# Attention into a token-mixing MLP: how p and the small weights are loaded, the form of the scores in batch 2, and the order of the work

## The chip, the cores and the metric

The kernel runs on one core of a Trainium2 chip. The metric is the device time of one execution in microseconds, as the median of several runs; a profiled execution gives the trace beside it. Engines are called PE (matrix products), DVE (vector), ACT (activation), POOL (GpSimd) and SP (which only issues transfers here). Transfers are issued by SP, ACT and POOL and run on 16 DMA engines that all of them share.

## The reference, cut to what matters

```python
def attn(qq, kk, vv):                      # scale = 1 / sqrt(64)
    s = scale * qq @ kk.T
    a = exp(s - max(s)); a = a / sum(a)
    return a @ vv

p_packed = attn(p, k, v)                   # p: 8 x 8 x 32 x 64, q, k, v: 8 x 8 x 576 x 64
x = heads_side_by_side(attn(q, p_packed, p_packed))      # 8 x 576 x 512
wq, wk = x @ w_q, x @ w_k                  # 512 x 64 each
mixed = (wq @ wk.T / sqrt(64)) @ x         # per batch, 576 x 576 mixing of tokens
out = maximum(mixed, 0) @ w_out            # 512 x 512, fp32
```

All inputs and the output are fp32. 32 learned vectors per head (p) attend to the keys and values, and the 576 queries then attend to the 32 results.

## The kernel before

All eight batches go through the same steps; nothing loops. The text `ORDER` is a list of steps, written out by hand or by a planner, and the program walks it once: `NAME.batch.piece@engine=banks`. The engine is V (DVE), A (ACT) or P (POOL); what follows `=` are the PSUM banks. Each engine runs its own steps in the order of the text and waits only for what a step reads, or for a buffer or bank that is still in use; the order between engines in the text has no further meaning. There are four buffers each for the loads of q, k and v, three for most of the rest, two for the exponentials. POOL's queue also shows waits of an issue for the landing of the eighth issue before it.

The steps of one batch, with the lines of the profile:

- `LD.k`, `LD.q`, `LD.v` (L184, L191, L181): 576 KB each in bf16, cast from fp32 on the way by POOL's transfers; v goes in two halves. `LD.g0` and `LD.h0` are the halves of k in batch 0, `LD.q7` and `LD.r7` those of q in batch 7. `LD.O` is w_out, `LD.W0` and `LD.W1` are w_q and w_k, `LD.P0` to `LD.P3` the four quarters of p. `LD.P0`, `LD.P1` and both W are fp32 copies on SP's or ACT's queue.
- At the start `PC` casts the two fp32 quarters of p (L137), `PX` transposes p (L244), `PB` spreads it into a block form for batches 0 to 2 (`pblk`), `WC` casts the two weights into `wqk`, and `SET` fills constants: ones beside v (L215), zeros of `pblk` (L218), the mask (L220), an identity (`idf`, `aff`, `idb`), zeros of `aT` (L140) and of the tile `warm`. `WARM.n` is n matmuls on that tile (L616), fillers whose result nobody reads.
- `KT` transposes k on DVE (L244). `S1` gives the scores of p against k. For the batches in `DIAG` they come with the tokens on partitions (L281, 36 matmuls with `pblk`), and one `X1` (L299) takes the exponential; for the others they come with p on partitions (L291, 32 matmuls), `X1` is two instructions (L302), and `TE` transposes the result back in two instructions on DVE (L244).
- `PV` (L318) multiplies with v and sums; `RC` and `PP` (L323, L327) divide; `PT` transposes the result, `QV` transposes q in three pieces (0, 1: 512 columns each, 2: the rest). `QK` (L340) and `QKE` give w_k and w_q times the packed values, `QD` copies a part on POOL.
- `S2` (L379) gives the scores of the queries, `X2` (L384) their exponential, `RS` and `RR` (L400, L405) the sums and reciprocals, `AM` (L411) the product of both on DVE or POOL, `AT` and `AE` the transposed result. Pieces 0 and 1 are two groups of 128 tokens each, 2 is the last, 3 is the first four groups and 4 all five. Batches 0, 1 and 7 use 0, 1 and 2, the others 3 and 2 (4 for the sums).
- `WKQ`, `WE`, `GM`, `GE`, `Y`, `YE`, `MX`, `MR`, `RL`, `RLR`: the token mixing, folded into small products, and the relu. `OT` (L546) is the product with w_out, `OE` and `OEF` bring it out of PSUM, `ST` (L564, L566) and `STF`, `STH` store it from SP. Results wait in SBUF: the first store stands in the text near the end of batch 6.
- `HOLD.q7` is a transfer of a few bytes from the second half of batch 7's q into a tile that nobody reads (L576). It stands last.

The core of the walk, and the first waits of the two forms:

```python
for item in ORDER.split():
    name, _, bk = item.partition("=")
    name, _, eng = name.partition("@")
    f = name.split(".")
    if f[0] == "LD":
        load(f[1], eng)
    ...
    steps[f[0]](*[int(z) for z in f[1:]], eng, bk[0] if bk and len(bk) == 1 else bk)
```

Of the kernel before, what the change touches and what calls it, by code (L numbers as in the profile page):

```python
# [29 lines left out]
AM.2.3@V AM.2.2@V AT.2.3=7 AT.2.2=6 AE.2.3@V RL.1.1@A AE.2.2@V TE.3.1@V OE.0.1@A TE.3.0@V KT.4.2@V  # L30
MR.1=2,3 OT.0.1 WKQ.2.0=0,1 WKQ.2.2 RLR.1@A OE.0.0@A MX.1.0=2,3 WKQ.2.1 PV.3.0=6,7 PV.3.1 RC.3.1@V
RC.3.0@V PP.3.0@V PP.3.1@V WE.2.2@A RL.1.0@A PT.3@V OT.1.4=4 S1.4=0,1,6,7 OEF.1.4@A QK.3=2
OT.1.0=4,5 GM.2=3 X1.4.1@A QKE.3@A X1.4.0@A QV.3.1@V QV.3.0@V QV.3.2@V S2.3.2=6,7 GE.2@A X2.3.2@A
S2.3.3=0,1 Y.2=6,7 TE.4.1@V TE.4.0@V YE.2@V X2.3.3@A RS.3.4@V OT.1.1 MR.2=6,7 PV.4.0=2,3 OE.1.0@A
RLR.2@A PV.4.1 MX.2.0=0,1 MX.2.1=4,5 OT.1.2=6,7 RL.2.0@A RL.2.1@A RR.3.4@V RC.4.0@V RC.4.1@V OT.1.3
# [17 lines left out]
OT.5.4=6 S2.7.2=2,3 S2.7.1=0,1 S2.7.0=4,5 X2.7.2@A OEF.5.4@V RS.7.2@V GM.6=7 X2.7.1@A RR.7.2@V
RS.7.1@V GE.6@A X2.7.0@A RS.7.0@V RR.7.1@V RR.7.0@V AM.7.0@V AM.7.1@V OT.5.2=2,3 QK.7=7 Y.6=4,5
AM.7.2@P AT.7.2=0 OT.5.3 QKE.7@A AE.7.2@A YE.6@A QD.7@P OE.5.1@A MX.6.0=4,5 MX.6.1=0,1 OT.5.0=6,7
AT.7.0=2 AT.7.1=3 AE.7.0@A RL.6.1@V RL.6.0@V AE.7.1@A OT.5.1 WKQ.7.0=0,1 WKQ.7.2 WKQ.7.1 OT.6.0=2,3
WE.7.0@V WE.7.1@A OE.5.0@V GM.7=0 OT.6.1 GE.7@V OE.6.0@A Y.7=6,7 MR.6=0,1 YE.7@V RLR.6@V OT.6.2=4,5
MX.7.0=2,3 MR.7=0,1 MX.7.1=6,7 RLF.7.0.0@A RLF.7.1.1@A RLR.7@V OT.6.3 RLF.7.0.1@V RLF.7.1.0@V
# [590 lines left out]
```

## Time and profile before

| | us |
|---|---|
| median of 3 runs (109.5 to 110.06) | 109.88 |
| the profiled execution | 109.32 |
| its span, first to last instruction | 107.5 |
| first product of data (S1.0) starts | 11.18 |
| last load lands | 79.1 |
| first store issued | 78.44 |
| PE's last product of batch 7 ends, ACT's last copy starts | 102.9 |

The span is what the trace shows; the execution's own time has 1.8 us around it. Times inside the trace are counted from the span's start. A row of the trace's time line reads: start, length, engine, line, operation, what it writes and reads, shape and type, and in brackets how long the engine had been idle before it and who released it. Matmuls are pipelined: PE's rows overlap, and a row's length is longer than its share of PE's time (a matmul of 512 columns has rows of 380 ns and follows the one before by 216).

The inputs are loaded in 37 transfers by POOL and four by SP and ACT; 14 of the stores are 512 KB each. The loads of batches 0 to 2 are issued by 17.8 us, those of batch 7 between 63.2 and 66.3.

### The profile page before, as it was taken

What the parts mean: (1) busy time and instruction counts of PE and PEld (TensorE: products, weight loads), DVE (VectorE), ACT (ScalarE), POOL (GpSimd) and SP (SyncE); (2) the same over time, 40 slices, a digit from 0 to 9 for tenths busy, and PEclk for the clock granted to TensorE, in tenths of its full rate; (3) what the DMA queues carried; (4) which work ended last, traced back from release to release, by engine and by line L of the source; (5) the groups of instructions that cost most, each with busy time, mean ns of one, the idle gap of its engine ahead of it and who ended that gap; (6) DMA issues with size and microseconds to landing.
All of it is one profiled execution on the core that took longest, in us unless ns stands there. A gap on an engine that the chain in (4) does not pass through costs nothing.

```text
span 107.5 us, 3632 instructions
## 1 busy us (share of the span) xinstructions
PE 97.2 (90%) x1551; PEld 54.8 (51%) x1551; DVE 82.8 (77%) x177; ACT 68.9 (64%) x108; POOL 42.7 (40%) x65
## 2 busy tenths in 40 slices
...
GB/s 41 196 145 172 213 214 210 207 213 217 203 208 214 204 209 213 209 207 214 208 214 206 214 205 211 213 209 208 162 115 396 407 393 401 395 405 329 213 370 120
DMA packets 13376, 25.01 MB, mean 233 GB/s; under 512 B 1072, under 2 KB 6448, under 8 KB 13360
## 3 DMA queue, kind: packets, MB, share of 16 engines
...
q8 instruction: 12, 0.20, 0.7%
...
HBM read 30.15 MB, written 9.44 MB: 368 GB/s over the span
## 4 chain that ended last, share of the span: by engine, by line
PE 68%; DVE 18%; ACT 5%; issue 3%; POOL 1%; DVEq 0%; ACTq 0%; POOLq 0%
PE ps L546 23%; PE ps L616 16%; PE ps L379 5%; PE ps L318 5%; PE ps L281 3%; ACT e L299 3%; PE ps L498 3%; DVE rs L400 3%; PE ps L425 3%; DVE kT L244 2%; PE ps L473 2%; PE ps L452 2%; DVE qT L244 2%; PE ps L291 2%; DVE aT L137 2%
## 5 line engine op out<-in xcount | busy, mean ns | idle before, releaser
L546 PE MATMUL ps<-wout,relu 128*128 128x512 bf16 x124 | 31.0, 380 | 0.6 <-DVE pp L327 0.6
L616 PE MATMUL ps<-o 128*128 128x512 bf16 x79 | 20.7, 410 | 3.6 <-DVE o L140 2.4
L411 POOL TENSOR_TENSOR a<-e,rr 128x256 bf16<-128x256 f32 (+2 forms) x11 | 13.1, 1196 | 23.4 <-DVE rr L405 23.4
L133 ACT ACTIVATE o<-ps 128x1024 f32<-128x1024 f32 (+2 forms) x18 | 15.7, 880 | 4.3 <-PE ps L546 3.9
L546 PEld LDWEIGHTS <-relu 128*128 128x128 bf16 x124 | 10.6, 98 | 11.9 <-issue 2.6
L384 ACT ACTIVATE e<-ps 128x256 f32<-128x256 f32 (+2 forms) x19 | 11.1, 620 | 7.7 <-PE ps L379 7.3
L509 ACT ACTIVATE relu<-ps 128x1024 bf16<-128x1024 f32 (+1 forms) x12 | 14.1, 1219 | 2.5 <-PE ps L498 2.1
L616 PEld LDWEIGHTS <-o 128*128 128x128 bf16 x79 | 7.6, 104 | 12.9 <-issue 3.9
L181 POOL DMA_DIRECT2D v_sb<-in_v_dram x16 | 10.1, 642 | 6.4 <-DMA q_sb<-in_q_dram 2.2
L244 DVE STREAM_TRANSPOSE qT<-q_sb 128x512 uint32<-128x512 uint32 (+1 forms) x24 | 12.4, 544 | 0.2 <-DMA q_sb<-in_q_dram 0.2
L244 DVE STREAM_TRANSPOSE kT<-k_sb 128x1152 uint32<-128x1152 uint32 (+1 forms) x9 | 11.0, 1224 | 1.3 <-DMA k_sb<-in_k_dram 1.2
L400 DVE TENSOR_REDUCE rs<-e 128x16 f32<-128x512 f32 (+2 forms) x13 | 10.8, 846 | 0.7 <-ACT e L384 0.6
L133 ACT ACTIVATE wkq<-ps 128x896 bf16<-128x896 f32 (+1 forms) x8 | 6.2, 776 | 3.7 <-PE ps L447 2.1
L318 PE MATMUL ps<-v_sb,e 64*64 64x192 bf16 x288 | 8.0, 245 | 0.1
L302 ACT ACTIVATE e1T<-ps 128x576 bf16<-128x576 f32 x10 | 6.4, 653 | 1.8 <-PE ps L291 1.8
L323 DVE RECIPROCAL rec<-ps 64x2 f32<-64x2 f32 x16 | 2.6, 164 | 6.2 <-PE ps L318 5.9
L244 DVE STREAM_TRANSPOSE e<-e1T 128x576 bf16<-128x576 bf16 x10 | 7.1, 744 | 0.0
L318 PEld LDWEIGHTS <-e 64*64 64x64 bf16 x288 | 6.0, 106 | 1.8 <-issue 1.0
L452 PE MATMUL ps<-aT,pqk 128*128 128x256 bf16 (+1 forms) x48 | 6.9, 246 | 0.0
L379 PE MATMUL ps<-ppT,qT 64*128 64x64 bf16 x320 | 6.4, 190 | 0.1
L379 PEld LDWEIGHTS <-qT 64*128 64x128 bf16 x320 | 5.4, 94 | 2.1 <-issue 1.1
L447 PE MATMUL ps<-pqk,aT 128*128 128x64 bf16 x80 | 6.1, 193 | 0.4 <-DVE aT L137 0.2
...
## 6 DMA issues: line engine op xcount, KB each, us to landing
...
v_sb<-in_v_dram POOLq DMA_DIRECT2D x16, 288.0 KB, 12.9
q_sb<-in_q_dram POOLq DMA_DIRECT2D x7, 576.0 KB, 13.4
k_sb<-in_k_dram POOLq DMA_DIRECT2D x7, 576.0 KB, 13.8
...
k_sb<-in_k_dram POOLq DMA_DIRECT2D x2, 288.0 KB, 6.9
q_sb<-in_q_dram POOLq DMA_DIRECT2D x2, 288.0 KB, 12.2
```

The lines of the kernel that those rows point to most:

```text
L133: nc.scalar.activation(o, i, COPY)
L181: nc.gpsimd.dma_start(v_bufs[b % NL][halves(i), 1:5], src)
L244: nc.vector.transpose(o, i)
L318: nc.tensor.matmul(T["pv", b][halves(cc), i, cc * Dh:(cc + 3) * Dh], lhsT, rhs, start=n == 0, stop=n == R - 1, skip_group_check=True)
L379: nc.tensor.matmul(ps[:, y, t - t0, i], lhsT, rhs, start=e == 0, stop=e == 1)
L384: nc.scalar.activation(e2[:, t0:t1].rearrange("a t (i y n) -> a y (t i) n", i=2, y=2), T["s2", b, c].rearrange("a y t i n -> a y (t i) n") ...
L400: nc.vector.tensor_reduce(rs[:, t0 * H:t1 * H], src, axis=AX, op=ADD)
L411: e.tensor_tensor(a2[:, t0:t1].rearrange("a t i (u l) -> a (t i u) l", l=L), e2v(b, c), T["rr", b][:, t0 * H:t1 * H].to_broadcast((P, (t1 ...
L452: nc.tensor.matmul(o, pqk[:, i, Dl:], aT[:, i, c0:c1], start=i == 0, stop=i == 1)
L509: nc.scalar.activation(o, i, RELU)
L546: nc.tensor.matmul(ps, lhsT, wout[:, j, :], start=j == 0, stop=j == NJ - 1)
L616: nc.tensor.matmul(ps, warm[:, 0:P], warm, start=True, stop=True)
```

## The change

- p: one quarter (`LD.P0`) comes in fp32 on ACT's queue, the other three (`LD.P1`) in one transfer of POOL that casts. `PC` casts half as much, on ACT. p's halves along L lie on other partitions than before, so `PX` writes with another pattern.
- w_q and w_k are cast in flight by POOL's transfers into `wqk`, which is laid out with the weight ahead of the parity; `WC` and the fp32 tile go. They now stand in POOL's queue behind v1 and behind q1.
- Batch 2 leaves `DIAG`: its scores come with p on partitions, with two `X1` and two `TE`. `pblk` shrinks to batches 0 and 1, and its second `SET` and four `PB` go.
- Batches 0 and 1 take their second attention in pieces 3 and 2, with one `RS` and one `RR` over all.
- The order is new throughout. `q0` comes in two halves; `pz0`, the mask and `v3` are filled by POOL; q follows v in batch 2; batch 7's v is loaded last; `HOLD.q7` stands ahead of the first store, on SP, and no longer at the end. The number of `WARM` matmuls goes from 79 to 84, 31 of them still in the first run.

```diff
-DIAG = (0,1,2)
+DIAG = (0,1)
...
-LD.P0@S LD.P1@S LD.P3 LD.P2 LD.W1@S SET.v0@V SET.v3@V SET.warm@V SET.pz0@V LD.g0 LD.h0 LD.v0 LD.q0
-SET.idf@V SET.aff@P LD.k1 SET.v2@P SET.tab@A PC@V SET.aT0@V PX@V SET.idb@V SET.mask@V KT.0.0@V
-PB.0.2@A LD.W0@A SET.pz1@V PB.1.2@V KT.0.1@V SET.v1@P LD.v1 LD.q1 PB.0.1@P LD.k2 PB.0.3@A PB.1.0@A
-PB.0.0@A WARM.31=1 S1.0=0,2,4 X1.0.0@A WARM.5=3 PV.0.0=0,1 PV.0.1 RC.0.0@V RC.0.1@V PP.0.1@V
-SET.aT1@V QV.0.2@V QV.0.1@V PP.0.0@V PT.0@V QV.0.0@V KT.1.2@V WARM.17=2 S2.0.2=0,1 S2.0.0=2,3
-S2.0.1=4,5 X2.0.0@A X2.0.2@A X2.0.1@A WC.0@A LD.q2 WARM.5=6 S1.1=2,3,4 PB.1.3@A X1.1.0@A RS.0.2@V
-RS.0.0@V RR.0.2@V AM.0.2@V PB.1.1@V WC.1@V WARM.3=0 QK.0=5 RR.0.0@V RS.0.1@V AM.0.0@V PV.1.0=2,3
-PV.1.1 AT.0.0=4 RC.1.1@V RC.1.0@V RR.0.1@V PP.1.0@V QV.1.0@V PP.1.1@V LD.v2 QKE.0@A AM.0.1@P QD.0@P
-LD.k3 AE.0.0@A WARM.6=5 AT.0.1=4 AT.0.2=5 WKQ.0.0=0,1 AE.0.2@V WKQ.0.2 WE.0.0@A AE.0.1@A SET.aT2@V
-PT.1@V QK.1=5 QV.1.1@V QV.1.2@V QKE.1@V KT.2.2@V WARM.1=6 S2.1.2=2,3 S2.1.1=6,7 WKQ.0.1 X2.1.2@A
-X2.1.1@A WE.0.1@V RS.1.2@V RS.1.1@V RR.1.2@V QV.2.2@V RR.1.1@V QV.2.0@V S2.1.0=2,3 X2.1.0@A RS.1.0@V
-RR.1.0@V AM.1.0@V WARM.5=6 GM.0=0 S1.2=1,2,3 GE.0@A X1.2.0@A QD.1@P LD.O LD.v3 AM.1.1@P Y.0=6,7
-YE.0@A WARM.4=4 AT.1.1=0 MX.0.0=6,7 MX.0.1=2,3 AE.1.1@V RL.0.1@A RL.0.0@A AT.1.0=1 PV.2.0=4,5 LD.k4
-QV.2.1@V AE.1.0@V PV.2.1 AM.1.2@P LD.q3 AT.1.2=0 RC.2.1@V RC.2.0@V AE.1.2@V PP.2.0@V PP.2.1@V
-MR.0=2,3 WKQ.1.0=0,1 WKQ.1.1 WKQ.1.2 PT.2@V S2.2.2=4,5 S2.2.3=6,7 RLR.0@A WE.1.0@A WE.1.1@V GM.1=0
...
-PP.4.1@V PP.4.0@V QV.4.0@V PT.4@V QV.4.2@V QV.4.1@V QK.4=0 QKE.4@V OE.1.1@A LD.v5 QD.3@P LD.q5
-AM.3.3@P LD.v6 AM.3.2@P QD.4@P AT.3.3=1 AE.3.3@V S2.4.2=4,5 X2.4.2@A S2.4.3=2,3 X2.4.3@A KT.5.2@V
-RS.4.4@V OT.2.2=6,7 AT.3.2=4 AE.3.2@A WKQ.3.0=0,1 WKQ.3.1 WKQ.3.2 WE.3.2@A S1.5=2,3,4,5 OT.2.3
-GM.3=1 RR.4.4@V X1.5.0@A GE.3@A OE.2.1@A X1.5.1@A OT.2.0=2,3 Y.3=0,1 OT.2.1 YE.3@A KT.6.2@V AM.4.2@V
-TE.5.0@V TE.5.1@V OE.2.0@A LD.q6 AM.4.3@P LD.k7 AT.4.2=4 AT.4.3=5 MX.3.0=0,1 MX.3.1=6,7 PV.5.0=2,3
-PV.5.1 AE.4.3@V RL.3.0@V AE.4.2@A RL.3.1@A WKQ.4.0=4,5 RC.5.1@V RC.5.0@V WKQ.4.1 WKQ.4.2
-S1.6=6,7,0,1 PP.5.1@V PP.5.0@V OT.3.0=2,3 OT.3.1 X1.6.0@A WE.4.2@A X1.6.1@A OE.3.0@A GM.4=4 PT.5@V
...
-OT.4.0=2,3 X2.6.3@A RLR.4@A KT.7.2@V RS.6.4@V S1.7=6,7,4,5 QKE.6@A AM.5.3@P QD.5@P AM.5.2@P QD.6@P
...
-RC.7.1@V PP.7.0@V PP.7.1@V AE.6.3@A ST.3.4 ST.2.0 ST.0.1 ST.1.4 ST.3.1 ST.2.1 ST.3.0 ST.0.0 ST.4.0
...
-OEF.7.0@A STF.7.1 STF.7.0 HOLD.q7
+LD.P0@A LD.h0 LD.P1 SET.aT1@V SET.warm@V SET.v2@V SET.v0@V SET.aT2@V SET.tab@A PC@A SET.aT0@V
+SET.pz0@P LD.g0 LD.v0 LD.r0 SET.idf@V KT.0.1@V PX@V PB.0.2@A PB.0.0@V PB.0.1@A PB.0.3@V KT.0.0@V
+LD.q0 SET.v1@P LD.k1 SET.mask@P LD.v1 SET.v3@P LD.W1 WARM.31=1 S1.0=0,2,4 X1.0.0@A WARM.5=3
+PV.0.0=0,1 PV.0.1 LD.q1 LD.W0 SET.aff@P LD.k2 RC.0.1@V RC.0.0@V PP.0.1@V PP.0.0@V SET.idb@V QV.0.0@V
+QV.0.2@V QV.0.1@V PT.0@V WARM.12=2 S2.0.2=0,1 S2.0.3=2,3 X2.0.3@A X2.0.2@A KT.1.2@V WARM.10=4
+S1.1=0,1,2 X1.1.0@A RS.0.4@V RR.0.4@V WARM.5=3 PV.1.0=4,5 PV.1.1 AM.0.3@V RC.1.0@V LD.v2 AM.0.2@P
+LD.q2 LD.k3 AT.0.2=0 RC.1.1@V PP.1.1@V WARM.8=2 QK.0=1 AT.0.3=2 QKE.0@A QV.1.0@V PP.1.0@V PT.1@V
+QV.1.2@V AE.0.2@V QV.1.1@V WARM.4=4 S2.1.2=0,1 AE.0.3@A S2.1.3=2,3 X2.1.2@A LD.O QD.0@P WKQ.0.0=0,1
+WKQ.0.1 WKQ.0.2 X2.1.3@A KT.2.2@V WARM.2=6 S1.2=2,3,4,5 RS.1.4@V WE.0.2@A X1.2.1@A X1.2.0@A GM.0=0
+GE.0@A WARM.4=1 Y.0=4,5 YE.0@A WARM.2=0 MX.0.1=2,3 QK.1=4 TE.2.1@V QKE.1@A RL.0.1@A RR.1.4@V
+MX.0.0=6,7 RL.0.0@A TE.2.0@V PV.2.0=0,1 QV.2.0@V LD.v3 LD.k4 LD.q3 AM.1.3@P AM.1.2@P PV.2.1 RC.2.1@V
+RC.2.0@V QV.2.2@V AT.1.3=5 PP.2.1@V PP.2.0@V QV.2.1@V PT.2@V MR.0=2,3 AT.1.2=4 S2.2.2=0,1 AE.1.3@A
+QD.1@P LD.v4 S2.2.3=6,7 X2.2.2@A AE.1.2@V X2.2.3@A KT.3.2@V RLR.0@V QK.2=5 WKQ.1.0=0,1 QKE.2@A
+WKQ.1.1 WKQ.1.2 WE.1.2@A S1.3=6,7,2,3 RS.2.4@V RR.2.4@V WARM.1=5 OT.0.2=4,5 GM.1=0 OT.0.3 AM.2.3@V
+QD.2@P LD.q4 AM.2.2@P LD.k5 X1.3.0@A X1.3.1@A GE.1@A Y.1=2,3 YE.1@V OE.0.1@A OT.0.0=0,1 MR.1=2,3
+MX.1.0=4,5 RL.1.0@A LD.q5 AT.2.2=6 OT.0.1 AT.2.3=7 TE.3.1@V TE.3.0@V RLR.1@V AE.2.3@V KT.4.2@V
...
+QV.4.1@V RL.2.1@A RL.2.0@A QK.3=2 QK.4=3 QKE.3@V KT.5.2@V QKE.4@V OE.1.0@A S2.4.2=0,1 S2.4.3=6,7
+X2.4.2@A X2.4.3@A AM.3.3@P AM.3.2@P QD.3@P LD.q6 QD.4@P LD.v6 RS.4.4@V RR.4.4@V AM.4.3@P AM.4.2@P
+LD.k7 LD.q7 LD.r7 AT.3.3=2 OT.2.2=0,1 AE.3.3@A S1.5=6,7,4,5 AT.3.2=3 OT.2.3 AE.3.2@A WKQ.3.0=2,3
+X1.5.0@A X1.5.1@A WKQ.3.1 WKQ.3.2 OT.2.0=4,5 WE.3.2@A OT.2.1 OE.2.1@A GM.3=3 OE.2.0@A QV.5.0@V
+TE.5.1@V TE.5.0@V QV.5.2@V QV.5.1@V GE.3@V AT.4.3=2 AE.4.3@V PV.5.0=0,1 Y.3=4,5 PV.5.1 YE.3@A
...
+RL.3.0@A WKQ.4.0=6,7 PT.5@V WKQ.4.2 WKQ.4.1 RL.3.1@V QK.5=1 WE.4.2@A S2.5.3=4,5 KT.6.2@V S2.5.2=2,3
+QKE.5@A GM.4=6 OT.3.0=0,1 GE.4@V X2.5.2@A X2.5.3@A S1.6=6,7,2,3 LD.v7 QD.5@P HA.5@P Y.4=4,5 X1.6.1@A
...
+S2.6.2=0,1 S2.6.3=6,7 X2.6.2@A AT.5.3=4 X2.6.3@A OT.4.0=0,1 AE.5.3@V OEF.3.4@A RS.6.4@V S1.7=6,7,2,3
+WKQ.5.0=4,5 X1.7.1@A HOLD.q7 WKQ.5.2 WKQ.5.1 X1.7.0@A OT.4.1 RR.6.4@V TE.7.1@V WE.5.2@A AM.6.2@P
+OT.4.2=6,7 TE.7.0@V AM.6.3@P OE.4.0@A ST.3.4 AT.6.2=4 GM.5=5 PV.7.0=2,3 AE.6.2@A GE.5@A QV.7.0@V
...
+OH.7.1=0 OT.7.2=6 OEH.7.0@A OEH.7.1@A OEF.7.4@A OEF.7.2@A STH.7.0 STH.7.1 ST.7.4 STF.7.2 OT.7.0=0
+OT.7.1=4 OEF.7.0@A STF.7.0 OEF.7.1@A STF.7.1
...
         elif a == "P":
-            c = int(b)
-            src = p.rearrange("b (i c) (y l) d -> c (b i) y (l d)", i=2, y=2)
-            if c > 1:
-                nc.gpsimd.dma_start(pbf[quarter(c)], src[c])
+            src = p.rearrange("b (i c) (y l) d -> (c y) (b i) (l d)", i=2, y=2)
+            if b == "1":
+                nc.gpsimd.dma_start(pbf[32:], src[2:])
             else:
-                (nc.sync if eng == "S" else nc.scalar).dma_start(p32[quarter(c)], src[c])
+                (nc.sync if eng == "S" else nc.scalar).dma_start(p32[0:32], src[0:2])
         elif a == "W":
-            w = (moe_w_q, moe_w_k)[int(b)].rearrange("(i c j e) m -> (c j) i (e m)", i=2, c=4, e=2)
-            (nc.sync if eng == "S" else nc.scalar).dma_start(w32[:, int(b)].rearrange("a i e m -> a i (e m)"), w)
+            w = (moe_w_k, moe_w_q)[int(b)].rearrange("(i c j e) m -> (c j) i (e m)", i=2, c=4, e=2)
+            nc.gpsimd.dma_start(wqk[:, :, int(b)].rearrange("a i e m -> a i (e m)"), w)
...
-        elif x == "r7":
-            nc.gpsimd.dma_start(q_in[7 % NL][:, 0], pairs(q, 7)[:, 0])
-        elif x == "q7":
-            nc.gpsimd.dma_start(q_in[7 % NL][:, 1], pairs(q, 7)[:, 1])
+        elif a == "r" or x in ("q0", "q7"):
+            b, i = int(b), int(a == "q")
+            nc.gpsimd.dma_start(q_in[b % NL][:, i], pairs(q, b)[:, i])
...
-    w32 = T["o"][NO - 2].rearrange("a t n -> a (t n)")[:, 0:8 * Dl].rearrange("a (w i e m) -> a w i e m", w=2, i=2, e=2)
...
     def PC(eng, bk):
-        copy(eng, pbf[0:64], p32[0:64])
+        copy(eng, pbf[0:32], p32[0:32])
 
     def PX(eng, bk):
-        blocks(pT.rearrange("a u (y l) e -> a (u y l e)", y=2).bitcast(u32).rearrange("a (u l) -> a l u", l=L // 2),
-               pbf.bitcast(u32).rearrange("a (l n) -> a l n", l=L // 2))
+        blocks(pT.rearrange("a u (y l) e -> a (u y l e)", y=2).bitcast(u32)
+               .rearrange("a (u y l) -> a l y u", y=2, l=L // 2),
+               pbf.bitcast(u32).rearrange("a (l y u) -> a l y u", l=L // 2, y=2))
...
-    def WC(n, eng, bk):
-        eng = eng or "P"
-        if n == 1:
-            copy(eng, wqk[:, :, :, 0], w32[:, 1])
-        else:
-            copy(eng, wqk[:, :, :, 1], w32[:, 0])
...
                     nc.tensor.matmul(ps[halves(y), i],
                                      T["ppT", b][halves(y), i, :, :, e].rearrange("a x l -> a (x l)"),
-                                     wqk[halves(y), i, e].rearrange("a x m -> a (x m)"),
+                                     wqk[halves(y), i, :, e],
                                      start=e == 0, stop=e == 1, skip_group_check=True)
...
     def hold(x):
         b = int(x[1])
-        src = {"k": k_in, "q": q_in, "r": q_in, "v": v_bufs}[x[0]][b % NL]
+        src = {"k": k_in, "h": k_in, "q": q_in, "r": q_in, "v": v_bufs}[x[0]][b % NL]
         src = src[64:96, 4, 0:2] if x[0] == "v" else src[64:96, 0 if x[0] == "r" else 1, 0:2]
-        nc.sync.dma_start(touch, src)
+        z = 2 * int(x[0] == "h")
+        nc.sync.dma_start(touch[:, z:z + 2], src)
```

More of the change, by code (lines that the diff above doesn't have):

```diff
@@ L30 @@
[L30 to L35, printed above, removed]
@@ L53 @@
[L53 to L58, printed above, removed]
@@ new lines @@
+MX.1.0=4,5 RL.1.0@A LD.q5 AT.2.2=6 OT.0.1 AT.2.3=7 TE.3.1@V TE.3.0@V RLR.1@V AE.2.3@V KT.4.2@V
+PV.3.0=2,3 MX.1.1=4,5 PV.3.1 AE.2.2@A OE.0.0@A RL.1.1@A OT.1.4=0 OEF.1.4@A RC.3.1@V RC.3.0@V LD.v5
+PP.3.0@V PP.3.1@V PT.3@V S1.4=6,7,4,5 WKQ.2.0=2,3 WKQ.2.1 WKQ.2.2 X1.4.1@A X1.4.0@A WE.2.2@A
+QV.3.0@V QV.3.2@V QV.3.1@V OT.1.2=4,5 S2.3.2=6,7 S2.3.3=2,3 X2.3.2@A TE.4.0@V TE.4.1@V GM.2=0
+X2.3.3@A OT.1.3 GE.2@V RS.3.4@V Y.2=2,3 PV.4.0=6,7 YE.2@A PV.4.1 OE.1.1@A MX.2.0=0,1 MX.2.1=2,3
+OT.1.0=4,5 RC.4.0@V RC.4.1@V RR.3.4@V LD.k6 OT.1.1 PP.4.0@V PP.4.1@V QV.4.0@V PT.4@V QV.4.2@V
```

34 lines of the change are left out of this document (18 added, 16 removed).

## The prediction

> **What bounds the kernel now.** I read the page's first lines, then the stages, then the chain of waits, then single transfers.
>
> ```profile
> span 107.5 us, 3632 instructions
> ...
> PE 97.2 (90%) x1551; PEld 54.8 (51%) x1551; DVE 82.8 (77%) x177; ACT 68.9 (64%) x108; POOL 42.7 (40%) x65
> ```
>
> 90% busy alone proves little: 79 of PE's matmuls are fillers on a dummy tile, and ends are modelled. The stages (length, busy time of each engine, clock, DMA share, GB/s) tell more:
>
> ```profile
> 2.00:10.40 8.40, 7.99 (x28) 3.25 (x29) 5.82 (x18) 1.41 (x6) 7.99 (x14) 1.00 0.99 170
> 10.40:33.80 23.40, 21.59 (x369) 12.70 (x368) 16.17 (x45) 9.28 (x18) 8.60 (x14) 1.00 1.14 211
> 33.80:79.10 45.30, 43.91 (x869) 25.62 (x867) 42.13 (x80) 39.06 (x59) 21.80 (x30) 1.00 1.11 202
> ...
> 81.00:97.00 16.00, 15.91 (x234) 9.19 (x234) 14.14 (x29) 10.91 (x18) 2.40 (x3) 1.00 1.02 399
> 97.00:101.00 4.00, 4.00 (x29) 2.14 (x29) 1.67 (x3) 3.37 (x6) 0.00 (x0) 1.00 0.57 226
> ```
>
> The DMA engines are full with loads to about 77 us (the last lands at 79.1) and with stores from 81 to 97; from 97 to 101 they run at 0.57, so at the end the stores wait for results, not the other way round. From 33.8 on PE is busy 97% and DVE 93%. The chain of waits agrees:
>
> ```profile
> 37.62 0.71 PE ps L379 x40
> ...
> 65.42 0.48 DVE relu L511
> 65.89 0.78 issue
> 66.67 0.17 DVE rec L323
> 66.85 0.17 DVE rec L323
> 67.05 0.62 DVE pp L327 x2
> 67.67 0.04 issue
> 67.72 1.89 PE ps L546 x8
> ...
> 101.16 1.74 PE ps L546 x8
> 102.93 0.60 ACT o L133
> ```
>
> The first line is S2.2. From it PE needs 65.3 us to its end at 102.9, nearly back to back; DVE shows as the releaser between 52 and 68. So I count in PE's order: when S2.2 starts, what PE has to do from there, what it stands still, and the tail. Before S2.2 PE waits for data and fills; time saved there counts only as far as S2.2 moves. Three transfers fix that (us from issue to landing; issued at 12.52, 17.20 and 65.67 on POOL):
>
> ```profile
> q_sb<-in_q_dram POOLq DMA_DIRECT2D x1, 576.0 KB, 18.4
> ...
> v_sb<-in_v_dram POOLq DMA_DIRECT2D x1, 288.0 KB, 16.6
> ...
> q_sb<-in_q_dram POOLq DMA_DIRECT2D x1, 288.0 KB, 13.4
> ```
>
> So q2 lands at 30.9, v2, the last input of batches 0 to 2, at 33.8, and the last of all at 79.1.
>
> **The change, part by part.**
>
> *Loads.* The bytes read are the same; the packet sizes change. In the trace's packet records a 2,304-byte packet takes 192 ns and a 1,152-byte one 107 ns: a line through both is 22 ns + 74 ns per KB. The cast weights are 2 x 256 packets of 256 bytes: 41 ns each by that line, over 16 engines 0.66 us per weight. Bounds: as a 4-byte packet (22 ns) 0.35 us, as a 1,152-byte one (107 ns) 1.7 us. Before, w_q stretched two v halves from 1.45 to 1.9 us each (0.9), and w_k's 256 packets at 28 ns took 0.45: 1.35 us, against 1.3 now (0.7 to 3.4). p: 64 packets of 4,096 bytes at about 200 ns and 64 cast ones at 245 ns were 1.8 us; 32 and 96 are 1.9. So the stream ends where it did: q2, now last of the three batches, lands at 33.7 (33.1 to 35.8).
>
> The Trainium skill (DMA: Bandwidth & Descriptors, Specifications) speaks against these casts: below 512 bytes a transfer is no longer at line rate, since the engine reads, modifies and writes. It gives no time; were each of the packets doubled to 82 ns, the estimate would be 2.6 us for both. The 512-byte fp32 packets of before stand at that limit, so no run here shows it yet.
>
> *Start.* P0 moves from SP to ACT's queue, in front of its table load (1.28 us); the rest of p waits behind h0 on POOL, and h0 is 8 packets per engine at 230 ns, 1.8 us. So PX moves from 5.4 to about 6.5. It is covered by the 31 fillers (8.84 us): they start once `warm` is zeroed, now after two 0.08 us memsets, at 1.4 instead of 2.4, and end at 10.2 instead of 11.2. Without that cover the later PX would cost 1.1 us. PC on ACT (1.02 us by the 1,024-column copies) ends before p lands. The memsets moved to POOL (pz0, mask, v3: about 1.5 us) stand ahead of g0, v1 and W1 in POOL's queue; the stream is 10 us deep there (k1: issued 5.88, landed 19.7), so I cost them at nothing; with no such backlog they cost 1.5 us. PB.1 (four copies) and WC (0.43 and 0.29) go. All of it lies ahead of k1, which sets KT.1: nothing.
>
> *Two pieces, and batch 2 in the other form.* For batches 0 and 1 DVE's sums and reciprocals go from 2 x 0.65 + 0.40 + 0.23 + 0.23 + 0.20 = 2.4 us to 1.47 + 0.40 = 1.9. Batch 2 adds TE.2 (2 x 0.72 on DVE), 2 x 0.65 instead of 1.13 on ACT, and 32 matmuls in 0.6 us instead of 36 in 1.2. From k2 (28.1): KT.2 to 30.2 as before, S1.2 30.9, X1.2 32.2, TE.2.1, RR.1 and TE.2.0 (1.84) to 34.1. Then q2 is there, and DVE has QV.2.0 0.70, RC 0.35, QV.2.2 0.26, PP 0.59, QV.2.1 0.70, PT.2 0.31 = 2.9 ahead of S2.2: it starts at 37.05 instead of 37.55. **-0.5** (-0.9 with an earlier stream, +1.3 if q2 lands at 35.8).
>
> *PE's work from S2.2 on.* WKQ.1 stood ahead of S2.2 and now follows it: 36.67 to 37.62 in the chain, 0.95; one filler less there, -0.22. Else both orders hold the same products. **+0.7**.
>
> *PE's standstills.* Two that name a releaser on DVE: 0.56 ahead of 67.72 (OT.3.0 waits until PP.5 has read banks 2, 3) and 0.22 ahead of 56.28 (QK.4 waits for PT.4). In the new order OT.3.0 follows S2.5 and GM.4, which need PT.5 anyway, and QK.4 has OT.1.0 and OT.1.1 (1.7 us) ahead of it. **-0.8**. A new order can open others; DVE's total from S2.2 on stays the same (60.9 to 60.6 us by the rows' means), so I take none, with -2 to +2 as bounds.
>
> *HOLD.q7.* It leaves the end, where the touch lands 0.2 us after the last store: **-0.2**. It now stands on SP ahead of ST.3.4, with every store behind it. q7 is third from last, three halves of 1.45 us ahead of 79.1, so 74.8; ST.3.4 waits for OEF.3.4 anyway, on ACT until 78.42 before. No cost; the pause of 97 to 101 covers 1.7 us more. v7 now lands last, some 1.4 us later; PV.7 (83.2 before) comes some 2 us earlier, and still behind it.
>
> *Sum:* -0.5 + 0.7 - 0.8 - 0.2 = -0.8 us. The profiled execution took 109.32 (span 107.5 and 1.8 around it): 108.5. The median of the runs is 0.56 above it: **109.1 us**.
>
> **Rivals.**
>
> *B, nothing left.* PE is full, the work is equal, and other waits take the place of the two: 109.1 + 0.8 = 109.9. For it: DVE is 93% busy in the middle whatever the order. Against: the two waits are tied to places that really move.
>
> *C, slower: the small casts hold up the stream.* W1 and W0 lie ahead of k2, v2 and q2 in the one load queue. At the 1,152-byte price they cost 3.4 us instead of 1.35, q2 lands at 35.8, S2.2 starts at 38.75, 1.7 later than in the sum: 110.8. It decides from q2 landing after 34.1. For it: q2 has become the last, with 2.9 us of DVE behind it. Against: the line through the packet sizes. Were the packets doubled as by the skill's rule above, q2 would land at 35.0 and the time be 110.0.
>
> *D, slower: POOL.* Batches 3 and 4 now send all four products (AM) to POOL, with QD.3, QD.4 and the issues of q6 and v6 between them. S1.5 to AT.4.3 is 4.4 us of PE work (AT.3.2, OT.2.3, WKQ.3, two OT, GM.3); on the other side QKE.4 0.4, RS.4 1.43, RR.4 0.40 and AM.4.3 1.91 = 4.1. Slack 0.3: every delay beyond it stops PE. An issue that waits for an earlier landing, as two did before (2.15 us at 17.20, 2.12 at 45.90), would cost 2.1 - 0.3 = 1.8: 110.9. Against: v6 would wait for v4, seven microseconds past by then.
>
> *E, more.* The first stage moved only 170 GB/s against 211. With p and the weights off the second queue it could keep 200: 8.4 x (200 - 170) / 211 = 1.2 us earlier; together with S2.2's chain 0.9 more than the sum, and a further stall of 0.4 gone: 107.8.
>
> **How the numbers follow.** The sum 0.42, B 0.17, C 0.15, D 0.17, E 0.09. Within 0.5% (109.33 to 110.43, what a measurement of this kernel can tell from no change) lie B and 0.05 of the sum: 0.22; faster 0.46, slower 0.32. The sum's own range is 108.2 to 109.8; to hold eight in ten across both signs it must reach E and past C and D: 107.3 to 111.4.
>
> **What would show it.** Right: fillers' first run ends near 10.2, S2.2 at 37.0 right behind PT.2, no idle ahead of OT.3.0 and QK.4, PE's end near 102, no touch behind the last store. Wrong: q2 landing after 34.1 (C), idle PE ahead of AT.4.3 with POOL as releaser (D), new waits on DVE elsewhere (B), or stores at full rate to the very end, which would put the bound on DMA.

## The result, and the profile after

The changed kernel takes **114.86 us** (median of 4 runs, 114.19 to 115.33); the kernel before took 109.69 beside it (108.98 to 110.06). The ratio is 1.0475, with a 95% interval of 1.0397 to 1.0552. The profiled execution took 114.19, its span is 112.1: 4.55 us more than before.

From the page of the changed kernel: its span, the engines' busy time, and from the 40 slices (2.8 us each) those of PE, of the granted clock and of DMA.

```profile
span 112.1 us, 3610 instructions
...
PE 97.7 (87%) x1552; PEld 54.4 (49%) x1552; DVE 78.5 (70%) x158; ACT 69.9 (62%) x101; POOL 48.3 (43%) x73
...
PE   5996159999999959999999998996899999999930
...
PEclk9999976999999999999999999999999999999998
DMA  0899999999999999999999999999339999995493
```

PE has its old amount of work (97.7 us against 97.2) in a longer span. Slices 5 and 6 are new: PE almost stands (1, then 5 tenths), and the clock falls to 7 and 6 tenths in slices 6 and 7. DMA falls to 3 tenths in slices 29 and 30, where the last loads land (81.54) and the first store starts (82.25).

The stages of the changed kernel, cut where PE's work changes: the run of fillers, the pause behind it, from S1.0 to S2.2, and from S2.2 to PE's end. The columns are the window, its length, the busy time of PE, PEld, DVE, ACT and POOL with instruction counts, the granted clock, the DMA share and GB/s.

```profile
2.00:10.40 8.40, 8.09 (x30) 3.18 (x28) 1.52 (x7) 2.54 (x3) 6.56 (x15) 1.00 0.89 143
10.40:13.67 3.27, 0.00 (x1) 0.00 (x1) 2.39 (x4) 0.83 (x2) 1.91 (x3) 1.00 1.17 204
13.67:41.42 27.75, 24.83 (x418) 14.04 (x419) 16.77 (x36) 12.09 (x17) 14.29 (x20) 0.94 1.15 198
41.42:107.50 66.08, 64.06 (x1103) 36.93 (x1102) 56.82 (x108) 53.86 (x80) 24.61 (x30) 1.00 0.98 248
```

The same for the kernel before, where no pause lies between the fillers and S1.0:

```profile
2.00:11.18 9.18, 8.77 (x31) 3.45 (x31) 6.55 (x18) 1.67 (x6) 8.65 (x15) 1.00 1.00 172
11.18:37.55 26.37, 24.11 (x434) 14.81 (x434) 18.70 (x53) 12.07 (x20) 11.01 (x17) 1.00 1.15 210
37.55:102.95 65.40, 64.31 (x1091) 36.58 (x1088) 56.59 (x105) 53.35 (x83) 22.13 (x29) 1.00 1.03 258
```

Counted by when PE starts a step (the last two columns are kernels of the experiments):

| us | before | after | a1_p16 | e1_pv2 |
|---|---|---|---|---|
| S1.0 starts | 11.18 | 13.67 | 10.42 | 10.24 |
| from there to S2.2 | 26.37 | 27.75 | 26.47 | 25.83 |
| from S2.2 to PE's last matmul | 64.96 | 65.64 | 66.15 | 64.98 |
| from there to the end of the span | 5.00 | 5.00 | 4.98 | 5.00 |

So of the 4.55 us, 2.49 are lost before S1.0, 1.38 between S1.0 and S2.2, 0.68 behind S2.2. The chain of waits names the first loss (start, length, what):

```profile
1.98 8.99 DMA o<-in_p_dram
...
11.07 1.06 DVE pT L239
...
13.67 1.26 PE ps L270 x36
```

Its time line shows who waits:

```profile
0.75 1.24 ACTq L168 DMA_DIRECT2D o<-in_p_dram  x1
...
1.98 0.65 POOL L166 DMA_DIRECT2D o<-in_p_dram  x1
...
5.93 1.06 ACT L131 ACTIVATE o<-o 32x1024 bf16<-32x1024 f32 x1 [2.41 <-DMA o<-in_p_dram]
...
11.07 1.05 DVE L239 STREAM_TRANSPOSE pT<-o 128x512 uint32<-128x512 uint32 x1 [3.01 <-DMA o<-in_p_dram]
11.26 0.62 POOL L178 DMA_DIRECT2D v_sb<-in_v_dram  x1 [2.53 <-DMA o<-in_p_dram]
...
13.67 1.24 PE L270 MATMUL ps<-pblk,kT 128*64 128x128 bf16 x36 [3.58 <-DVE kT L239]
...
16.13 2.29 PE L606 MATMUL ps<-o 128*128 128x512 bf16 x5 [1.22 <-ACT e L288]
```

PC waits 2.41 us for P0, PX 3.01 us for P1. PX starts at 11.07 instead of 5.44, S1.0 comes 2.6 behind it, and PE stands 3.58 us. POOL's issue of v1's second half is held too, 2.53 us, by the same landing. The step that releases PE is KT.0.0, which stands behind PX and two PB on DVE and starts at 12.84. Its input, the k half g0, landed only at 12.49 (9.07 in a1_p16 below), so an earlier PX alone would have won at most 0.35 us (an estimate from these two times): p came late itself, and k came late as well. The five fillers behind the pause take 2.29 us, 0.43 each from start to start, where they follow by 0.216 otherwise.

The profiled execution is the fastest of the four. In c3_am5 below, which starts with the same steps, S1.0 to S2.2 took 28.64 us instead of 27.75, with S1.0 itself at 2.13 instead of 1.24: the part of the slow clock differs from run to run.

The issue rows (size of one, median time from issue to landing) give the cause a size. Before:

```profile
o<-in_p_dram SPq DMA_DIRECT2D x2, 128.0 KB, 3.0
...
o<-in_p_dram POOLq DMA_DIRECT2D x2, 64.0 KB, 3.0
```

After:

```profile
o<-in_p_dram POOLq DMA_DIRECT2D x1, 192.0 KB, 9.0
o<-in_p_dram ACTq DMA_DIRECT2D x1, 128.0 KB
```

(P0's landing has no record; PC's start at 5.93 stands for it.) The packets are as large as before and take no more time each: P0's 32 take 195 ns in the mean (198 for fp32 before), P1's 96 also 195 (259 for the cast ones before). But P0's 32 packets take 3.27 us from the first to the last, with never more than 3 under way, where the 64 of before took 1.82 with up to 19; P1's 96 take 5.83 us with at most 9 under way. In the mean 32 x 0.195 / 3.27 = 1.9 of P0's are under way. P1's last 21, from 8.13 on, also run 1.9 at a time. In c1_p0 below, where P0 is out of the way, P1's 96 take 2.90 us at 179 ns each: 5.9 in the mean. P0 reads `src[0:2]` and P1 `src[2:]` of an array whose first dimension is (c y): the outermost dimensions of the two transfers are 2 and 6, where the four transfers of before had 16 rows outermost.

The Trainium skill states the rule (DMA: Bandwidth & Descriptors, the section on why a DMA increments its semaphore by 16): a transfer uses the largest number of engines, up to 16, that divides the slowest dimension (other than 1) of both its access patterns; it names an exception for some copies that GpSimd issues. By the rule P0 (2 rows, 32 partitions) runs on two engines and P1 (6 rows, 96 partitions) on six. The traces agree, with 1.9 and 5.9 packets under way in the mean. The most at any time, 3, 9 and 19, lie somewhat above 2, 6 and 16. That P0 and P1 are single transfers is not the reason: h0 is one too and has up to 18 packets under way.

### The profile page after: what moved, and what is told of

It is laid out like the page before. It is cut to its first block, busy times and chain, and to the rows that moved or that the text cites. A ratio compares the mean times of both kernels' runs of the same rounds, so it can differ in the third digit from the quotient of the medians.

```text
span 112.1 us, 3610 instructions
## 1 busy us (share of the span) xinstructions
PE 97.7 (87%) x1552; PEld 54.4 (49%) x1552; DVE 78.5 (70%) x158; ACT 69.9 (62%) x101; POOL 48.3 (43%) x73
## 4 chain that ended last, share of the span: by engine, by line
PE 66%; DVE 11%; DMA 8%; ACT 7%; issue 3%; POOL 1%; DVEq 0%; POOLq 0%
PE ps L535 25%; PE ps L606 9%; DMA o<-in_p_dram 8%; PE ps L368 6%; PE ps L307 5%; PE ps L414 3%; PE ps L487 3%; PE ps L441 3%; ACT relu L498 2%; PE ps L462 2%; PE ps L270 2%; PE ps L436 2%; DVE kT L239 2%; PE ps L329 2%; DVE rec L312 2%
## 5 line engine op out<-in xcount | busy, mean ns | idle before, releaser
L400 POOL TENSOR_TENSOR a<-e,rr 128x256 bf16<-128x256 f32 (+2 forms) x12 | 16.1, 1355 | 28.5 <-DVE rr L394 23.1
L606 PE MATMUL ps<-o 128*128 128x512 bf16 x84 | 23.0, 422 | 2.5 <-DVE o L138 1.3
L131 ACT ACTIVATE o<-ps 128x1024 f32<-128x1024 f32 (+2 forms) x19 | 16.8, 892 | 3.2 <-PE ps L535 2.9
L498 ACT ACTIVATE relu<-ps 128x1024 bf16<-128x1024 f32 (+1 forms) x13 | 15.4, 1232 | 1.7 <-PE ps L487 1.6
L606 PEld LDWEIGHTS <-o 128*128 128x128 bf16 x84 | 8.2, 106 | 12.5 <-issue 4.7
L178 POOL DMA_DIRECT2D v_sb<-in_v_dram x16 | 10.1, 638 | 6.1 <-DMA k_sb<-in_k_dram 3.0
L389 DVE TENSOR_REDUCE rs<-e 128x40 f32<-128x1280 f32 (+2 forms) x9 | 10.5, 1178 | 2.9 <-ACT e L373 2.9
L239 DVE STREAM_TRANSPOSE e<-e1T 128x576 bf16<-128x576 bf16 x12 | 8.5, 739 | 0.0
L368 PEld LDWEIGHTS <-qT 64*128 64x128 bf16 x320 | 6.1, 94 | 4.0 <-issue 1.8
L291 ACT ACTIVATE e1T<-ps 128x576 bf16<-128x576 f32 x12 | 7.1, 649 | 0.7 <-PE ps L280 0.7
L400 DVE TENSOR_TENSOR a<-e,rr 128x1024 bf16<-128x1024 f32 (+2 forms) x5 | 6.1, 1227 | 0.1
```

What stands on the lines that cost most here:

```text
L131: nc.scalar.activation(o, i, COPY)
L178: nc.gpsimd.dma_start(v_bufs[b % NL][halves(i), 1:5], src)
L239: nc.vector.transpose(o, i)
L368: nc.tensor.matmul(ps[:, y, t - t0, i], lhsT, rhs, start=e == 0, stop=e == 1)
L389: nc.vector.tensor_reduce(rs[:, t0 * H:t1 * H], src, axis=AX, op=ADD)
L400: e.tensor_tensor(a2[:, t0:t1].rearrange("a t i (u l) -> a (t i u) l", l=L), e2v(b, c), T["rr", b][:, t0 * H:t1 * H].to_broadcast((P, (t1 ...
```

## The experiments

Every kernel was timed beside the kernel before; each ratio is to that, with its 95% interval.

**a1_p16: the changed kernel, p in four transfers with 16 rows outermost.** PX goes back to its old pattern.

```diff
-src = p.rearrange("b (i c) (y l) d -> (c y) (b i) (l d)", i=2, y=2)
+src = p.rearrange("b (i c) (y l) d -> c (b i) y (l d)", i=2, y=2)
-    nc.gpsimd.dma_start(pbf[32:], src[2:])
+    nc.gpsimd.dma_start(pbf[quarter(c)], src[c])
-LD.P1
+LD.P1 LD.P2 LD.P3
```

> The changed kernel with p loaded quarter by quarter as before the change (one fp32 quarter on ACT, three cast ones on POOL), each with 16 rows as the outermost source dimension; order otherwise the same. Theory 'few engines' (p's two transfers of the change have 2 and 6 as outermost dimension and ran on 2 and 6 of the 16 DMA engines, p landed at 11.0 and these engines lagged from then on): p lands by 7, S1.0 starts near 10.3 instead of 13.7, the third batch's q lands near 33.8 instead of 36.0, S2.2 starts near 37 instead of 41.4, and the time is 108.5 to 110.5. Rival 'order' (the new order holds S2.2 by itself, p's lateness is hidden by the fillers): S2.2 stays after 40 and the time above 113.

Measured: 109.63 us, ratio 1.0006 (0.9979 to 1.0033). P lands at 3.54, 5.48, 5.81 and 6.18, and up to 19 of its cast packets are under way at once. From its time line:

```profile
3.56 1.06 ACT L131 ACTIVATE o<-o 32x1024 bf16<-32x1024 f32 x1 [0.63 <-DMA o<-in_p_dram]
...
6.31 1.04 DVE L240 STREAM_TRANSPOSE pT<-o 128x512 uint32<-128x512 uint32 x1 [0.35 <-DMA o<-in_p_dram]
...
10.42 1.24 PE L270 MATMUL ps<-pblk,kT 128*64 128x128 bf16 x36
```

PX at 6.31 is what the prediction had (6.5), S2.2 at 36.89 too (37.05), and q2, behind both small casts, lands at 33.3. The few engines cost 5.2 us, as much as the whole loss.

**b1_pnew: the kernel before, with the change's loads of p alone,** and the PC and PX that go with them.

```diff
-LD.P0@S LD.P1@S LD.P3 LD.P2
+LD.P0@S LD.P1
```

> The kernel before with the change's loads of p alone (one quarter on SP with 2 as outermost source dimension, three in one cast with 6). 'Few engines': 96 cast packets on 6 engines are 16 each at 0.2 us, so p lands near 6.5 to 7.5 instead of 4.9, these engines lag by some 2 us through the whole stream (last load near 81 instead of 79.1), S1.0 starts near 13 and the time is 111 to 113. 'Order': p's later landing is covered by the 31 fillers, 109.5 to 110.3.

Measured: 115.18, ratio 1.0492 (1.0426 to 1.0559): more than expected. P1 lands 8.8 us after its issue, at 10.19 and not by 7.5, PX starts at 10.29, S1.0 at 14.01, the last load lands at 82.95 instead of 79.1. The change's p loads alone make the whole loss in the other order too.

**a2_warm: the changed kernel with 50 instead of 31 fillers in the first run,** so that PE does not stand.

> The changed kernel with 50 fillers in the first run instead of 31, so that PE does not stand idle from 9.7 to 13.7. It tells the clock's part from the data's part: after the idle stretch matmuls followed each other at 0.43 us instead of 0.216 for a while. 'Few engines' with the clock as its smaller part: S1.0 at 13.7 to 14, the first PV about 1 us earlier than 18.35, time 113.5 to 114.8. If the clock were the larger part: 111 to 112.

Measured: 114.37, ratio 1.0399 (1.0326 to 1.0472). The window from 16 to 20 us, of the changed kernel and then of this one:

```profile
16.00:20.00 4.00, 3.87 (x44) 1.82 (x44) 0.30 (x2) 0.08 (x1) 2.31 (x4) 0.64 1.17 204
```

```profile
16.00:20.00 4.00, 2.87 (x45) 1.61 (x46) 0.65 (x4) 0.92 (x1) 2.30 (x4) 1.00 1.19 205
```

The clock stays at 1.00 instead of 0.64, and S1.0 to S2.2 takes 26.47 instead of 27.75. But the fillers end late, S1.0 starts at 14.49 (expected by 14), the first PV comes only 0.2 earlier, and S2.2 0.46. The pause's clock is the smaller part: 1.3 us in the profiled execution of the changed kernel, 2.2 by the trace of c3_am5, part of it taken back here by the longer run. The two kernels' intervals overlap, so this rests on the stages and not on the times.

**b2_wcast: the kernel before with w_q and w_k cast in flight,** behind v1 and q1 as in the change, without WC.

> The kernel before with w_q and w_k cast in flight, behind v1 and q1 in POOL's queue, and without the two copies that cast them. 'Few engines' and 'order': the 256-byte packets take 41 ns each, 0.66 us per weight, about what the fp32 copies cost: 109.3 to 110.3. Rival 'small casts': the stream is held up, 111 or more.

Measured: 110.68, ratio 1.0077 (1.0045 to 1.0109), above the expected range. The packets of 256 bytes take 41 ns in the mean, as predicted, and not the doubled 82, which was an estimate of the prediction's own (42 and 45 for the two weights in the changed kernel). The loss is one of place:

```profile
11.71 0.70 POOL L174 DMA_DIRECT2D wqk<-in_moe_w_k_dram  x1 [0.99 <-DMA v_sb<-in_v_dram]
12.46 0.39 POOL L135 COPY pblk<-pT 32x256 bf16<-32x256 bf16 x1
12.90 1.27 PE L281 MATMUL ps<-pblk,kT 128*64 128x128 bf16 x36 [1.63 <-POOL pblk L135]
```

PB.0.1 stands on POOL behind the issue of W0, which waited 0.99 us for an earlier landing; it started at 10.04 before, and S1.0 at 11.18. The changed kernel has PB.0.1 on ACT, so this does not explain its loss. That the casts do not hold its stream is borne out by a1_p16, where they are the same and q2 lands at 33.3.

**c1_p0 and c2_p1: which of the two transfers?** The changed kernel with only P0, or only P1, cut into transfers of 16 rows.

```diff
# c1_p0
-nc.scalar.dma_start(p32[0:32], src[0:2])
+for n in range(2):
+    nc.scalar.dma_start(p32[16 * n:16 * n + 16], src[n])
# c2_p1
-nc.gpsimd.dma_start(pbf[32:], src[2:])
+for n in range(2, 8):
+    nc.gpsimd.dma_start(pbf[16 * n:16 * n + 16], src[n])
```

> The changed kernel, with P0 alone cut into two transfers of 16 rows each (same bytes, same packets, same places in SBUF); P1 stays one transfer with an outermost dimension of 6. Few engines, with P1 as the part that decides: P0 lands at about 3.5 us instead of 5.9, but PX stays behind P1 at 9.5 to 11, and the time falls by at most 1 us, to 113.8 to 115. Rival, the fp32 quarter on two engines is what decides: PX near 6.5 and 110 to 111 us.

> The changed kernel, with P1 alone cut into six transfers of 16 rows each; P0 stays one transfer with an outermost dimension of 2. Few engines, with P1 as the part that decides: P1's last piece lands at 6 to 7.5, PX starts at 7 to 8, covered by the fillers, and the time is 110 to 111.3 us (two engines still carry P0's 32 packets and lag a little behind). Rival, P0 decides: PX stays at 9.5 to 11 and the time above 113.

Measured: c1_p0 111.06, ratio 1.0131 (1.0068 to 1.0195), and c2_p1 111.68, ratio 1.0202 (1.0148 to 1.0256). My view that P1 decides was wrong: each cut takes back more than half. With P0 cut, P1, still on its six engines, lands at 7.84 instead of 10.97 and h0 at 5.26 instead of 7.26. P0's 16 packets per engine had stood ahead of both, which fits P0's two engines lying among P1's six, and P1's last packets running 1.9 at a time; the trace does not number engines, so that is inferred. With P1 cut, its pieces land by 8.56 and P0 still holds PC until 6.32. This kernel pays for the cut as well: six issues, and POOL's first v0 waits 2.1 us for h0. In both kernels S1.0 (11.38 and 11.40) waits for KT.0.0, and that for g0, which lands at 10.52 and 10.54 instead of 9.07: what p leaves behind in the load stream. So the two do not add; both transfers had to be mended.

**d2_late: late p, but on all engines.** a1_p16 with P1 to P3 behind g0 on POOL.

> The changed kernel with p in four transfers of 16 rows (109.63 us), but the three of them on POOL issued behind g0, so that PX comes late while every transfer still uses 16 engines. If what cost the time is the lag of the few engines in the load stream, PX at 9 to 10.5 costs little: q2 lands at 33 to 34, S2.2 starts at 37 to 37.5, and the time is 109.6 to 110.4. If the lateness of PX by itself is the cost: S2.2 above 39.5 and 112 to 114 us.

Measured: 111.32, ratio 1.0139 (1.0072 to 1.0207): between the two.

```profile
9.24 1.04 DVE L240 STREAM_TRANSPOSE pT<-o 128x512 uint32<-128x512 uint32 x1 [3.42 <-DMA o<-in_p_dram]
...
11.73 1.26 PE L270 MATMUL ps<-pblk,kT 128*64 128x128 bf16 x36 [0.92 <-DVE kT L240]
```

q2 lands at 33.56, as in a1_p16 (33.32), and yet S2.2 starts at 38.20, 1.31 later: exactly the 1.31 by which S1.0 is later. From S1.0 to S2.2 it is 26.47 us, as in a2_warm (26.48 in c1_p0) and in a1_p16:

```profile
10.42:36.89 26.47, 23.12 (x413) 13.63 (x419) 17.01 (x36) 12.09 (x17) 15.42 (x22) 1.00 1.16 207
```

So in these kernels the loads are not what S2.2 waits for; PE's sequence from S1.0 on, fillers included, has a fixed length, and whoever delays S1.0 delays the end. The length is a least one. In c2_p1 it is 27.73 at a clock of 1.00: PE stands there 0.61 us within PV.0 for v0, whose second half lands at 15.88.

**e2_few: the changed kernel with 12 fewer fillers between S2.0 and S2.1.**

```diff
-WARM.10=4
+WARM.2=4
...
-WARM.8=2
+WARM.4=2
```

> The changed kernel as it is, with 12 fewer fillers between S2.0 and S2.1 (10 to 2 ahead of S1.1, 8 to 4 ahead of QK.0; the output does not depend on them). Theory: PE's order from S1.0 to S2.2 has a fixed length of some 26.5 us, padded for a start near 10.4, so a late S1.0 is carried on one to one although k1 and k2 have long landed; with fewer fillers part of it is made good: S1.1 near 23.8, S2.2 at 38.9 to 39.9 instead of 41.4, and 112.4 to 113.5 us. Rival, the lagging loads set S2.2: S2.2 above 40.8 and 114.2 to 115.2 us.

Measured: 113.88, ratio 1.0406 (1.0357 to 1.0456), in neither range. S2.0 to S2.2 takes 17.57 us instead of 18.88, so 1.3 of the 2.6 us of fillers were padding. Most of the rest covered a true wait: ahead of S1.1 PE now stands 0.85 us for the exponential of S2.0. S2.2 starts at 40.90, not by 39.9; that is the rival's side of its line (40.8), but not by the rival's cause: q2 lands at 36.42, and DVE's transpose of it starts at 37.10 behind other work, without a wait for it. The interval overlaps that of the changed kernel; direction and stage fit, the size is half of what I gave.

**c3_am5: the standstill behind S2.2.** In the changed kernel two products of batch 5 run side by side:

```profile
76.57 1.91 POOL L400 TENSOR_TENSOR a<-e,rr 128x1024 bf16<-128x1024 f32 x1 [2.09 <-DVE rr L394]
...
77.00 1.76 DVE L400 TENSOR_TENSOR a<-e,rr 128x256 bf16<-128x256 f32 x1
...
78.82 0.23 PE L409 MATMUL ps<-idb,a 128*128 128x64 bf16 x2 [1.24 <-DVE a L400]
```

Before, DVE's product of 128x256 ran alone in 0.42 us:

```profile
22.13 0.42 DVE L411 TENSOR_TENSOR a<-e,rr 128x256 bf16<-128x256 f32 x1
```

Here it takes 1.76, ends 0.28 us after POOL's, and PE stands 1.24 us ahead of AT.5.2. The kernel before had such a pair too, AM.4.2 beside AM.4.3: 1.21 us from 62.28 on, but PE did not stand for it. The edit is `AM.5.2@P AM.5.3@P` for `AM.5.2@V AM.5.3@P`.

> The changed kernel, with AM.5.2 on POOL ahead of AM.5.3 instead of on DVE beside it. Theory: DVE's product of 128x256 took 1.76 us there (0.42 when it ran alone) because POOL's product ran beside it, and PE stood 1.2 us ahead of AT.5.2 for it. Moved, AT.5.2's input is there some 0.6 us after rr.5, the standstill goes, and the time falls by 0.8 to 1.3 us, to 113.6 to 114.1 (ratio to before 1.035 to 1.040). Rival, DVE is full in that stage and another wait takes its place: within 0.3 us of 114.86.

Measured: 113.89, ratio 1.0438 (1.0365 to 1.0510): the time is as expected, but the interval overlaps that of the changed kernel, so the stage has to show it. Both products now run on POOL, and AT.5.2 starts without a wait of PE:

```profile
77.49 2.49 POOL L400 TENSOR_TENSOR a<-e,rr 128x256 bf16<-128x256 f32 x2 [2.13 <-DVE rr L394]
...
78.31 0.22 PE L409 MATMUL ps<-idb,a 128*128 128x64 bf16 x2
```

S2.2 to PE's last matmul takes 64.32 instead of 65.64. The Trainium skill has this rule (SBUF — State Buffer, the section on SBUF's two separate sides): a DVE operation with two inputs from SBUF and a GpSimd operation that reads SBUF share a pair of ports, and the one that starts first keeps it for its whole instruction. The traces agree with 0.42 against 1.76, and the other way round: at 26.77 POOL's 128x256 product, started 0.13 us behind DVE's of 1.23 us, took 1.58 instead of 0.61.

**c4_p16_am5: both mends.**

> Both mends: p in four transfers of 16 source rows each (109.63 us alone) and AM.5.2 on POOL. If the two losses are separate, they add: 108.3 to 108.9 us, ratio to before 0.987 to 0.993. If another wait takes the place of the standstill: 109.4 to 109.8.

Measured: 108.86, ratio 0.9919 (0.9883 to 0.9955). They add: 0.77 below a1_p16.

**d1_wkq: c4_p16_am5 with two thirds of WKQ.1 ahead of S2.2,** where PE stands 1.1 us, and other banks to make room (GM.1 goes from bank 0 to 6 too).

```diff
-S2.2.2=0,1 AE.1.3@A QD.1@P LD.v4 S2.2.3=6,7 X2.2.2@A AE.1.2@V X2.2.3@A KT.3.2@V RLR.0@V QK.2=5 WKQ.1.0=0,1 QKE.2@A WKQ.1.1 WKQ.1.2 WE.1.2@A S1.3=6,7,2,3
+AE.1.3@A QD.1@P WKQ.1.0=6,7 WKQ.1.1 S2.2.2=0,1 LD.v4 X2.2.2@A AE.1.2@V S2.2.3=4,5 WKQ.1.2 X2.2.3@A KT.3.2@V RLR.0@V QK.2=0 WE.1.2@A QKE.2@A S1.3=0,1,2,3
```

> Both mends as before (p in transfers of 16 rows, AM.5.2 on POOL: 108.86 us), and of WKQ.1 the first two thirds put back ahead of S2.2, into the 1.3 us in which PE waits for PT.2 (banks of S2.2.3, QK.2, S1.3 and GM.1 moved to make room). If the prediction's term of +0.7 us for WKQ.1 behind S2.2 is real, S2.2 starts where it did (36.9 to 37.4) and the time falls by 0.4 to 0.7 us, to 108.2 to 108.5. Rival, DVE is the bound behind S2.2 and the time saved on PE turns into waits: 108.7 to 109.

Measured: 111.77, ratio 1.0199 (1.0135 to 1.0263), a miss; neither theory had seen it:

```profile
33.69 2.49 ACT L498 ACTIVATE relu<-ps 128x1024 bf16<-128x1024 f32 x2
...
36.01 1.04 ACT L131 ACTIVATE aT<-ps 128x1024 bf16<-128x1024 bf16 x1
...
37.10 0.29 PE L436 MATMUL ps<-pqk,aT 128*128 128x64 bf16 x4 [1.64 <-ACT aT L131]
```

WKQ.1 reads aT of batch 1, which ACT copies only behind two relu copies; PE stood 1.64 us for it with S2.2 queued behind, and 1.64 more ahead of S1.3, whose bank QK.2 now held until ACT's `QKE.2`. In this order WKQ.1 belongs behind S2.2.

**e1_pv2: c4_p16_am5 with PV.2 ahead of QK.1 and MX.0.0.**

```diff
-MX.0.1=2,3 QK.1=4 TE.2.1@V QKE.1@A RL.0.1@A RR.1.4@V MX.0.0=6,7 RL.0.0@A TE.2.0@V PV.2.0=0,1
+MX.0.1=2,3 TE.2.1@V RL.0.1@A RR.1.4@V TE.2.0@V PV.2.0=0,1
...
-PV.2.1
+PV.2.1 QK.1=4 QKE.1@A MX.0.0=6,7 RL.0.0@A
```

> Both mends (p in transfers of 16 rows, AM.5.2 on POOL: 108.86 us, ratio 0.992), and PV.2 moved ahead of QK.1 and MX.0.0 in PE's order, so that DVE's chain RC.2, QV.2.2, PP.2, QV.2.1, PT.2 can begin 0.7 us earlier; PE stands 1.3 us for that chain ahead of S2.2. If the chain from PV.2 sets S2.2: S2.2 starts some 0.6 us earlier and the time falls by 0.2 to 0.6 us, to 108.3 to 108.7. Rival, ACT's copies (relu.0, QKE.1, AE.1.3), now moved behind it, set what follows S2.2: no change, 108.7 to 109.0.

Measured: **108.32** us, ratio 0.9888 (0.9846 to 0.9929), below both kernels; the interval overlaps that of c4_p16_am5, so what PV.2's place is worth is read from the stage. Its stages, then its first S2.2:

```profile
10.24:36.07 25.83, 23.42 (x419) 13.67 (x419) 17.01 (x36) 11.77 (x17) 15.11 (x23) 1.00 1.16 207
36.07:101.50 65.43, 64.26 (x1103) 37.19 (x1102) 55.31 (x107) 53.99 (x80) 25.59 (x32) 1.00 1.04 259
```

```profile
36.07 0.78 PE L368 MATMUL ps<-ppT,qT 64*128 64x64 bf16 x40 [0.61 <-DVE ppT L240]
```

S1.0 to S2.2 is 25.83 instead of 26.47 in a1_p16, and PE's wait for PT.2 0.61 instead of 1.1: the chain from PV.2 over DVE did set S2.2.

## Why the prediction was wrong, by its own steps

- *Loads.* This is the failing step. "32 and 96 are 1.9" us divides p's packets by 16 engines: (32 x 200 + 96 x 245 ns) / 16. The number of packets was right, and the fp32 ones' length (195 ns for about 200; the cast ones took 195 and not 245). The number of engines was 2 and 6, and P1 took 5.83 us from its first packet to its last. I read the sizes of the packets out of the diff, and not the order of the dimensions. "So the stream ends where it did" fell with it: q2 lands at 36.02, the last load at 81.54. With 16 engines q2 lands at 33.32 (predicted 33.7), which bears out the price of the casts, 41 ns a packet.
- *Start.* "PX moves from 5.4 to about 6.5" became 11.07; on 16 engines it is 6.31. "Covered by the 31 fillers" held to PX at about 7.5 (they end at 10.1, and S1.0 comes 2.6 after PX), and PX missed that by more than 3 us.
- "All of it lies ahead of k1, which sets KT.1: nothing" and "three transfers fix that" were wrong for this order, whatever p does: d2_late shows that S2.2 follows S1.0 one to one with k2, v2 and q2 in time. I had counted fillers as slack; in this order they are work of a fixed length.
- *Two pieces, and batch 2 in the other form.* S2.2 at 37.05 was predicted and 36.89 measured once p ran on 16 engines: the number was right, in part by luck. q2 came 0.4 earlier than predicted, but DVE then stood 0.92 us for PV.2: the chain that sets S2.2 began at PV.2 on PE and not at q2 (e1_pv2).
- *Work and standstills from S2.2 on.* +0.7 and -0.8 were to cancel; measured is +0.68. The waits ahead of OT.3.0 and QK.4 are gone as predicted. New ones took their place: 1.24 us ahead of AT.5.2, of a kind that I had not looked for, an operation moved to DVE beside one of POOL, and 0.30 ahead of MX.3.1. c3_am5 takes the first back and comes to 64.32, 0.64 less than before where the sum had 0.1 less; no run explains the other 0.5.
- *HOLD.q7.* Nothing of the -0.2 shows: PE's last matmul to the end of the span is 5.00 us in both. At its new place it cost nothing that shows: the first store waits for OEF.3.4 until 82.25.
- *Rivals.* C's condition came true (q2 after 34.1), but not from the casts, and S2.2 did not wait for it: DVE's transpose of q2 starts at 37.63, 1.6 us after q2 landed. D's place, AT.4.3, shows no wait; POOL's mishap was another one. B, a new wait in place of the old, is what happened behind S2.2. E's first stage moved 143 GB/s and not 200. That a transfer could run on few engines was not among the rivals, so the range missed by 3.5 us.
- Without p's fault it is 109.63 for a predicted 109.1. What is left is above all the standstill ahead of AT.5.2: without that too (c4_p16_am5) it is 108.86. a1_p16 also stands 0.34 us for w_out, which lands at 39.95.

In the changed kernel S1.0 to S2.2 took 1.28 longer than 26.47. All of it lies ahead of S2.0: from S1.0 to there it took 8.87 us at a clock of 0.81, where a1_p16 took 7.57 at 1.00, and from S2.0 to S2.2 18.88 against 18.90. So the late loads (k1 at 21.66, q2 at 36.02) added nothing behind S2.0; a2_warm, with loads as late and the clock up, has 26.47. Open is the price of the casts' place in b2_wcast, which was not run with PB.0.1 elsewhere.
